# An mLSTM cell and a leaky-ReLU MLP on one core: another order at the start of each MLP group, an earlier weight load, and weight sums at other places

## The chip, the cores and the metric

The kernel runs on one core of a Trainium2 chip. A core has several engines that run side by side, each with its own queue in program order: PE (TensorE, matrix products; its weight loads are shown as PEld), DVE (VectorE), ACT (ScalarE), POOL (GpSimd) and SP (SyncE, which here only issues DMAs; ACT issues some too). They hand work to each other through semaphores. Data lie in SBUF, products in PSUM, the inputs and the output in device memory (HBM).

The metric is the device time of one execution in microseconds (us); the median of several executions counts. One further execution was recorded by the hardware profiler; all times inside the kernel are from it.

## The reference

Two blocks in a row, all in float32. The first is an mLSTM cell over 4 batches, 8 heads, 768 steps, 40 values per head. The second multiplies its output, as 3072 rows of 320, by two matrices with a leaky ReLU between them.

```python
for t in range(S):                       # first block
    m_new = np.maximum(f_gate[:, :, t] + m, i_gate[:, :, t])
    f_stab = np.exp(f_gate[:, :, t] + m - m_new)
    i_stab = np.exp(i_gate[:, :, t] - m_new)
    C = f_stab[..., None, None] * C + i_stab[..., None, None] * np.einsum('bhd,bhe->bhde', vt, kt)
    n = f_stab[..., None] * n + i_stab[..., None] * kt
    denom = np.maximum(np.abs(np.einsum('bhd,bhd->bh', n, qt)[..., None]), 1.0)
    y[:, :, t] = sigmoid(o_gate[:, :, t]) * np.einsum('bhde,bhe->bhd', C, qt) / denom
x = y.transpose(0, 2, 1, 3).reshape(3072, 320)
h = x @ w_in                             # second block: 320 x 2048
out = np.maximum(0.01 * h, h) @ w_out    # 2048 x 320
```

## The kernel before

**Chunks and groups.** The 768 steps are cut into 6 chunks of 128. Within a chunk the cell is computed with matrix products, batch by batch; one batch of one chunk is called a cell here, numbered s = 4 * chunk + batch. What the cells of chunk g give (4 batches x 128 steps = 512 rows of x) is the input of MLP group g. The main loop (variable `c`, 1 to 6) runs the products of group c - 1 and, between them, the cells of chunk c. It steps through 28 products for a group from 1 on (index `i`); after each product it lets other work in. The queues of PE, DVE, ACT and POOL hold exactly the order in which this loop calls things; a planner places only SP's DMAs.

**The cell's visits.** A cell visits PE twice: `u_parts` (scores `sd`, lines 629 and 634, followed on DVE by L639 and L610) and `u_mix` (product `pT`, L710, followed by a row on DVE and POOL: L717, L648 to L650, L721 on DVE, L724 on POOL, L728 on DVE). The list `pairs` says after which `i` the visits of two cells come. Before its visits a cell needs its mask added (`prep_mask`, POOL L453), exponentials (`prep_exp`, ACT L461), transposes and products of k and q (`prep_kq`, DVE L516 and L524), and steps of the state on POOL (L606, L481). The gates of the next chunk are scanned on DVE (`gates`, L283 to L303) and put through exponentials on ACT (`gates_exp`, L314 and L315).

**The fast groups.** Groups 1 to 5 use a scheme that replaces 8 block products by 7 with sums of blocks. For the first layer (`fast_firsts`) the blocks are those of x (b11, b12, b21, b22; b12 and b22 hold the second half of the rows) and of w_in. The products are p1, p6, p7, p4, p2, p5, p3, each for n = 0 and 1. p1, p6 and p7 have two terms, the others three. A product accumulates in two PSUM banks; p1, p6, p7, p4 follow each other in the same banks ("u"), p2 has its own ("s"), p5 and p3 share a third pair ("v"). After a product ACT copies the banks to `acts` (L979) or DVE adds them to it (L975), and ACT applies the leaky ReLU (L971). A product that goes on in a bank has to wait until this reading is over. Group 1 alone has p2 ahead of p1 (`swapped`). The sums of x (`sums_of_x`) are 12 instructions on POOL (L928). The sums of w_in (`sums_of_weights`) are 14 on DVE (L908 to L911, L918), once.

The second layer (`fast_units`, L830) has its own seven products, also called p1 to p7, in the order p1, p2, p4, p6, p7, p5, p3. They use four sums of blocks of w_out (`mixed_weights`, POOL L203 to L206, 128x1280 each), made once, in group 1. In this document p1 to p7 mean the first layer's products unless the second layer is named.

**Weights.** w_in and w_out come from HBM as 64-bit words, two eighths or quarters at a time, into a staging area, and are narrowed to float32 by seven instructions (`narrow_weights`: ACT L251, then DVE L253 to L267). The last eighth of w_out is loaded at `i` = 15 of c = 1 into a part of the staging area that an earlier eighth used.

Of the kernel before, what the change touches and what calls it, by code (L numbers as in the profile page):

```python
# [10 lines left out]
U32 = mybir.dt.uint32  # L11
# [7 lines left out]
def kernel(  # L19
# [176 lines left out]
    x4_at = raw_l[:, at + 12 * P : at + 12 * P + 2 * HT].rearrange("p (k t) -> p k t", t=HT)  # L196
    p1_at = [raw_l[:, at + 12 * P + 2 * HT + n * NH :][:, :NH] for n in range(2)]

    def mixed_weights():

        a11, a12, a21, a22 = low_w[:, :, :NH], low_w[:, :, NH:], high_w[:, :, :NH], high_w[:, :, NH:]
        t2, t3, t4 = t_at
        yield nc.gpsimd.tensor_tensor(t3, a22, a12, op=ALU.subtract)  # L203
        yield nc.gpsimd.tensor_tensor(a12, a12, a11, op=ALU.subtract)
        yield nc.gpsimd.tensor_tensor(t2, a22, a12, op=ALU.subtract)
        yield nc.gpsimd.tensor_tensor(t4, a21, t2, op=ALU.subtract)  # L206

    def load_weights(n):

        m = n - QN  # L210
        if n < QN:
            dst = w_in[:, n, :]
        else:
            dst = w_out[:, 2 * m : 2 * m + 2, :].rearrange("p a d -> p (a d)")
        to = dst
        if wide:
            if n < 2:
                at = NF * GT - 2 * WC * (n + 1)
                raw = acts_l[:, at : at + 2 * WC].bitcast(U64)
            elif n < QN:  # L220
                raw = raw_t[:, WC * (n - 2) : WC * (n - 1)]
            elif m < 2:
                raw = w_out[:].rearrange("p f d -> p (f d)")[:, (2 + m) * WC : (3 + m) * WC].bitcast(U64)
            else:
                at = (4, 0, 1, 2, 3, 4)[m - 2] * HW
                raw = raw_t[:, at : at + HW]
            raws[n] = (raw, dst)
            to = raw
        if n < QN:
            src = moe_w_in[:, n * QC : (n + 1) * QC].rearrange("(k p) (r c) -> r p k c", p=DP, r=2)  # L230
            for slot in range(KC):
                for r in range(2):
                    nc.sync.dma_start(  # L233
                        to[DP * r : DP * (r + 1), 2 * P * slot : 2 * P * (slot + 1)], src[r, :, SLOTS[r][slot], :],
                    )
        else:
            rows = moe_w_out[2 * m * P : 2 * (m + 1) * P, :]
            nc.sync.dma_start(to.rearrange("p (a d) -> p a d", d=Dm), rows.rearrange("(a p) d -> p a d", p=P))

    def narrow_weights(n):  # L240
# [6 lines left out]
        words = raw.bitcast(U32).rearrange("p (c two) -> p c two", two=2)  # L247
        lo, hi = words[:, :, 0], words[:, :, 1]
# [671 lines left out]
    def sums_of_x(g):  # L920

        xT = st["xT", g]
        for what in range(4):
            for rows, k, a, b in alike:
                b11, b12, b21, b22 = (xT[rows, j, ts(i, HT)] for j in (a, b) for i in range(2))
                x2, x3, x4 = (t[rows, k] for t in (x2_at, x3_at, x4_at))
                to, left, right = ((x3, b22, b12), (b12, b12, b11), (x2, b22, b12), (x4, b21, x2))[what]
                nc.gpsimd.tensor_tensor(to, left, right, op=ALU.subtract)  # L928

    def fast_firsts(g):  # L930
# [50 lines left out]
        swapped = g == 1  # L981

        def p1(n):
            z = at(n, 0, 0)
            bank = product(n, list(zip(w_at(0, n, K1), x_at(K1, 0))), ("u", n))
            if swapped:
                add(z, bank)
                relu(z, z)
            else:
                keep(z, bank)  # L990
# [7 lines left out]
        def p4(n):  # L998
            bank = product(n, list(zip(w_at(1, n, K2), t_of(x4_at))) + rest(1, n, 0), ("u", n))
# [3 lines left out]
        def p2(n):  # L1003
            z = at(n, 0, 0)
            bank = product(n, list(zip(w_at(0, n, K2), x_at(K2, 0))) + rest(0, n, 0), ("s", n))
            if swapped:
                keep(z, bank)
            else:
                add(z, bank)
                relu(z, z)  # L1010

        def p5(n):
            z = at(n, 1, 1)
            add(z, product(n, list(zip(w_at(1, n, K1), x_at(K1, 1))) + rest(1, n, 1), ("v", n)))
# [7 lines left out]
        order = (p2, p1, p6, p7, p4, p5, p3) if swapped else (p1, p6, p7, p4, p2, p5, p3)  # L1022
        return [lambda p=p, n=n: p(n) for p in order for n in range(2)]
# [23 lines left out]
    def ahead(s):  # L1047

        if s < NS:
            if s < 2 * B:  # L1050
                u_split(s)
            if s >= 2 * B:
                late[s] = 5 if 2 * B + 2 <= s < 3 * B else 3
# [114 lines left out]
    with tc.manual_schedule(engines={E.PE, E.DVE, E.Activation, E.Pool}):  # L1168
# [23 lines left out]
        for c in range(1, NB + 1):  # L1192
# [6 lines left out]
            for i in range(n_ff):  # L1199
# [102 lines left out]
```

## Time and profile before

| | |
|---|---|
| median of 3 executions | 502.8 us (502.01 to 503.71) |
| profiled execution | 496.93 us |
| its span, first to last instruction | 495.1 us |
| mean granted PE clock | 0.972 |
| PE busy | 480.3 us (97%) |
| DVE busy | 353.7 us (71%) |
| ACT busy | 203.7 us (41%) |
| POOL busy | 199.8 us (40%) |
| HBM traffic | 118 GB/s over the span |

Busy time is the time in which an engine executes instructions; waits and DMA issues are not counted. The profile's windows cut the span into stretches and give each engine's busy time in them, with the clock that PE was granted (1.00 is full). The list of waits says who waited for whom. The order of time lists instructions with start and length; "x3" are three in a row under one line.

The five fast groups start at 138.78, 216.89, 288.20, 359.45 and 430.17 us in the span. Ahead of them lie the first chunk's cells, the narrowing of the weights and group 0.

### The profile page before, as it was taken

Reading aid. Unit: us, or ns where it says so; the run is one execution under the profiler, and the core shown is the slowest. Engines: PE = TensorE matmul, PEld = TensorE weight load, DVE = VectorE, ACT = ScalarE, POOL = GpSimd, SP = SyncE. Lnnn points to the kernel's source line nnn. Section 1 sums busy time; section 2 is a strip of 40 time slices with the busy share of each in tenths; the row PEclk is TensorE's granted clock in tenths of the full one; section 3 lists DMA queues with packets and bytes.
Section 4 is the critical chain, followed back from the end, with each engine's and each line's share of the span. In section 5 each row is a group of like instructions: output and inputs, shape, how many; then the busy total and the mean of one; then the engine's idle time right before and its main releaser. Section 6 shows DMA issues by size and latency. Waiting matters only on the chain.

```text
span 495.1 us, 14022 instructions
## 1 busy us (share of the span) xinstructions
PE 480.3 (97%) x5621; PEld 433.5 (88%) x5621; DVE 353.7 (71%) x585; ACT 203.7 (41%) x508; POOL 199.8 (40%) x239
## 2 busy tenths in 40 slices
PE   8997999999998899999999999999999999999997
PEld 7896788867787789998899998899989899988997
DVE  4759998898999967786787886787737787104641
ACT  3465865742635351155631335620344611153210
POOL 4142743452385961494412694203583003700020
PEclk9568999999999989999999999999999999999999
DMA  9977786898761573486584685663865211200001
GB/s 115 161 193 160 168 209 163 173 187 169 158 142 26 135 149 80 115 167 151 145 152 96 150 170 118 174 124 93 156 161 128 54 56 46 87 1 1 2 1 54
DMA packets 165297, 59.31 MB, mean 120 GB/s; under 512 B 128816, under 2 KB 156016, under 8 KB 165232
## 3 DMA queue, kind: packets, MB, share of 16 engines
q1 hardware_dynamic: 125104, 51.20, 46.0%
q10 hardware_dynamic: 40128, 7.21, 9.2%
q8 instruction: 44, 0.72, 0.6%
q14 instruction: 21, 0.17, 0.1%
HBM read 51.68 MB, written 6.70 MB: 118 GB/s over the span
## 4 chain that ended last, share of the span: by engine, by line
PE 70%; DVE 11%; SPq 9%; DMA 4%; ACT 3%; issue 2%; POOL 0%; ACTq 0%; DVEq 0%; POOLq 0%
PE po L830 31%; PE ph L946 27%; SPq L233 4%; PE pT L710 3%; PE sd L629 2%; PE po L796 2%; SPq L358 2%; PE ph L774 2%; DVE qn L524 1%; SPq L372 1%; DVE qn L639 1%; ACT kqT L554 1%; PE sd L634 1%; DMA w<-a_dr 1%; DMA rb<-in_q_dram 1%
## 5 line engine op out<-in xcount | busy, mean ns | idle before, releaser
L830 PE MATMUL po<-w_out,acts 128*128 128x160 f32 x640 | 89.1, 300 | 0.0
L830 PEld LDWEIGHTS po<-w_out,acts 128*128 128x128 f32 x640 | 87.3, 190 | 0.6 <-ACT acts L971 0.3
L946 PE MATMUL ph<-xT,w_in 64*128 64x256 f32 x720 | 82.7, 378 | 0.0
L946 PEld LDWEIGHTS ph<-xT,w_in 64*128 64x128 f32 x720 | 69.2, 187 | 8.9 <-issue 0.7
L975 DVE TENSOR_TENSOR acts<-acts,ph 128x512 f32<-128x512 f32 x60 | 38.3, 682 | 41.6 <-PE ph L946 41.5
L830 PE MATMUL po<-raw,acts 128*128 128x160 f32 x480 | 66.4, 300 | 0.0
L830 PEld LDWEIGHTS po<-raw,acts 128*128 128x128 f32 x480 | 65.4, 190 | 0.3
L606 POOL TENSOR_TENSOR S<-S,f 40x336 f32<-40x336 f32 x36 | 31.6, 879 | 75.7 <-PE pT L710 35.9
L461 ACT ACTIVATE w<-w,gT 128x64 f32<-128x64 f32 (+1 forms) x192 | 51.7, 346 | 15.7 <-DMA w<-a_dr 4.6
L979 ACT COPY acts<-ph 128x512 f32<-128x512 f32 x60 | 32.1, 587 | 46.7 <-PE ph L946 46.7
L971 ACT ACTIVATE acts<-acts 128x1024 f32<-128x1024 f32 x30 | 31.7, 1056 | 43.6 <-DVE acts L975 43.4
L774 PE MATMUL ph<-xT,w_in 64*128 64x256 f32 x320 | 38.6, 392 | 1.2 <-ACT acts L782 1.2
L946 PE MATMUL ph<-acts,w 64*128 64x256 f32 x320 | 37.5, 382 | 1.8 <-DVE acts L975 1.8
L453 POOL TENSOR_TENSOR w<-w,i 128x512 f32<-128x512 f32 x20 | 27.7, 1394 | 26.2 <-DMA w<-a_dr 14.3
L774 PEld LDWEIGHTS ph<-xT,w_in 64*128 64x128 f32 x320 | 31.6, 193 | 5.7 <-ACT acts L782 1.6
L796 PE MATMUL po<-w_out,acts 128*128 128x320 f32 x128 | 36.5, 437 | 0.0
L946 PEld LDWEIGHTS ph<-acts,w 64*128 64x128 f32 x320 | 31.2, 187 | 5.7 <-POOL w L453 2.2
L724 POOL TENSOR_TENSOR xb<-xb,den 128x320 f32<-128x320 f32 x16 | 11.6, 727 | 60.5 <-DVE xb L721 58.1
L639 DVE TENSOR_TENSOR qn<-w,sd 64x512 f32<-64x512 f32 x40 | 27.3, 684 | 8.2 <-PE sd L629 4.5
L796 PEld LDWEIGHTS po<-w_out,acts 128*128 128x128 f32 x128 | 23.6, 190 | 9.3 <-issue 0.3
L863 POOL TENSOR_TENSOR y<-y,raw 128x160 f32<-128x160 f32 x10 | 9.5, 950 | 54.5 <-DVE acts L865 44.0
L946 PE MATMUL ph<-xT,raw 64*128 64x256 f32 x240 | 29.0, 394 | 1.7 <-DVE acts L975 1.7
(169 smaller groups left out, 810.8 us busy)
## 6 DMA issues: line engine op xcount, KB each, us to landing
rb<-in_k_dram SPq DMA_DIRECT2D x64, 80.0 KB
rb<-in_q_dram SPq DMA_DIRECT2D x64, 80.0 KB
rb<-in_o_gate_dram SPq DMA_DIRECT2D x64, 80.0 KB
ea<-a_dr SPq DMA_DIRECT2D x32, 128.0 KB
raw<-in_moe_w_out_dram SPq DMA_DIRECT2D x6, 640.0 KB
w<-a_dr ACTq DMA_DIRECT2D x24, 128.0 KB
xT<-x_dr SPq DMA_DIRECT2D x32, 96.0 KB
acts<-in_moe_w_in_dram SPq DMA_DIRECT2D x20, 128.0 KB
```

What stands on the lines that cost most here:

```text
L233: nc.sync.dma_start(to[DP * r : DP * (r + 1), 2 * P * slot : 2 * P * (slot + 1)], src[r, :, SLOTS[r][slot], :],)
L453: nc.gpsimd.tensor_tensor(w, w, cm2.unsqueeze(1).to_broadcast([P, H, SL]), op=ALU.add)
L461: yield nc.scalar.activation(w[:, h, :], w[:, h, :], AF.Exp, bias=gT[c][:, 0, bh : bh + 1], scale=1.0)
L606: nc.gpsimd.tensor_tensor(new, old, g, op=ALU.mult)
L639: nc.vector.tensor_tensor(mixed(s)[toks, u], w[toks], bank[1 - u][toks], op=ALU.mult)
L774: nc.tensor.matmul(ph[r][:, cols], lhsT=w_row(r, slot, j), rhs=xT[DP * r : DP * (r + 1), slot, cols], start=(slot == 0), stop=(slot == KC ...
L796: nc.tensor.matmul(po[n][:], lhsT=acts[:, f, ts(n, P)], rhs=w_out[:, f, :], start=(f == 0), stop=(f == NF - 1),)
L830: nc.tensor.matmul(bank[:], lhsT=left[:, f, :], rhs=right[:, f, :], start=f == 0, stop=f == KH - 1)
L946: nc.tensor.matmul(bank[r][:, e, :], lhsT=left(r)[rows, e], rhs=right(r)[rows], start=first and e == 0 and m == 0, stop=e == 1 and m == le ...
L971: nc.scalar.activation(to, z, AF.Prelu, alpha=0.01)
L975: nc.vector.tensor_tensor(to[:, 2 * r : 2 * r + 2], to[:, 2 * r : 2 * r + 2], bank[r], op=ALU.add)
L979: nc.scalar.copy(to[:, 2 * r : 2 * r + 2], bank[r])
```

## The change

- The last eighth of w_out is loaded at `i` = 11 instead of 15, into the unused upper halves of `w_all`, as two DMAs of half the columns each. `narrow_weights` follows with a three-dimensional view.
- All fast groups begin with p2, then p1; p2 is copied by ACT and p1 added by DVE. Before, this held for group 1 alone.
- The sums of x write b12 - b11 to an area of its own (`x1_at`) instead of over b12, in another order, nine ahead of the group. The last three (b21 minus a sum, over b21) are issued behind p2(1) (`last_sum_of_x`), since p2 reads b21.
- The first two cells' `u_parts` come at `i` = 0 instead of 1; `gates` at `i` = 3 and `gates_exp` at 4 for all chunks from the third (c = 3 and later had 0 and 2). The masks of the third and fourth cell move from `i` = 0 to 4.
- The mixed weights of w_out: three of the four stay on POOL, at `i` = 0 (two) and 1 of group 1 instead of from 10 on; the fourth (a12 - a11) goes to DVE at `i` = 18.
- The last two sums of w_in (L918) come behind the gates of group 1.
- ACT's slow DMA issues (`chores`) start at `i` = 8, one per product, and two per product from 14. The steps of `prep_kq` go one per product up to 13 and two after it, in all groups.

```diff
-    x4_at = raw_l[:, at + 12 * P : at + 12 * P + 2 * HT].rearrange("p (k t) -> p k t", t=HT)
+    x1_at = raw_l[:, at + 12 * P : at + 12 * P + 2 * HT].rearrange("p (k t) -> p k t", t=HT)
...
         yield nc.gpsimd.tensor_tensor(t3, a22, a12, op=ALU.subtract)
-        yield nc.gpsimd.tensor_tensor(a12, a12, a11, op=ALU.subtract)
-        yield nc.gpsimd.tensor_tensor(t2, a22, a12, op=ALU.subtract)
+        yield nc.gpsimd.tensor_tensor(t2, t3, a11, op=ALU.add)
         yield nc.gpsimd.tensor_tensor(t4, a21, t2, op=ALU.subtract)
+        yield nc.vector.tensor_tensor(a12, a12, a11, op=ALU.subtract)
...
+            elif m == NF // 2 - 1:
+                raw = w_all[:, :, H * SL :].bitcast(U64)[:, :, : HW // NL]
+                dst = dst.rearrange("p (n c) -> p n c", n=NL)
...
-                at = (4, 0, 1, 2, 3, 4)[m - 2] * HW
+                at = (4, 0, 1, 2, 3)[m - 2] * HW
...
+            if len(to.shape) == 3:
+                n = NL // 2
+                for a in range(2):
+                    nc.sync.dma_start(to[:, n * a : n * (a + 1), :], rows[ts(a, P), :].rearrange("p (n c) -> p n c", n=n))
+                return
...
-        for what in range(4):
+        for what in range(3):
             for rows, k, a, b in alike:
-                b11, b12, b21, b22 = (xT[rows, j, ts(i, HT)] for j in (a, b) for i in range(2))
-                x2, x3, x4 = (t[rows, k] for t in (x2_at, x3_at, x4_at))
-                to, left, right = ((x3, b22, b12), (b12, b12, b11), (x2, b22, b12), (x4, b21, x2))[what]
+                b11, b12, b22 = xT[rows, a, :HT], xT[rows, a, HT:], xT[rows, b, HT:]
+                x1, x2, x3 = (t[rows, k] for t in (x1_at, x2_at, x3_at))
+                to, left, right = ((x1, b12, b11), (x2, b22, x1), (x3, b22, b12))[what]
                 nc.gpsimd.tensor_tensor(to, left, right, op=ALU.subtract)
+
+    def last_sum_of_x(g):
+
+        for rows, k, a, b in alike:
+            b21 = st["xT", g][rows, b, :HT]
+            nc.gpsimd.tensor_tensor(b21, b21, x2_at[rows, k], op=ALU.subtract)
...
-        order = (p2, p1, p6, p7, p4, p5, p3) if swapped else (p1, p6, p7, p4, p2, p5, p3)
-        return [lambda p=p, n=n: p(n) for p in order for n in range(2)]
+        return [lambda p=p, n=n: p(n) for p in (p2, p1, p6, p7, p4, p5, p3) for n in range(2)]
...
-                late[s] = 5 if 2 * B + 2 <= s < 3 * B else 3
+                late[s] = 5 if s % B > 1 else 3
...
-        fetch = {4: (3, 4), 8: (5, 6), 15: (7,)}
+        fetch = {4: (3, 4), 8: (5, 6), 11: (7,)}
...
-        masks = {0: (2, 3), 12: (4, 5)}
-        pairs = (1, 1, 4, 4, 13, 13, 17, 17, 17)
-        sums = sums_of_weights()
+        masks = {4: (2, 3), 12: (4, 5)}
+        pairs = (0, 0, 4, 4, 13, 13, 17, 17, 17)
+        sums, mixes = sums_of_weights(), mixed_weights()
...
-                for _ in range(1 if c > 2 and i < N1 else 2 if i > 5 else 0):
+                for _ in range(1 if i < N1 else 2):
...
-                if c == 1 and i >= 24:
+                if c == 1 and 24 <= i < 28:
                     run(sums, 3)
-                if c == 2 and i == 10:
-                    mixes = mixed_weights()
-                if c == 2 and i >= 10:
-                    next(mixes, None)
+                if c == 2 and i in (0, 1, 18):
+                    run(mixes, 2 if i == 0 else 1)
...
-                if chores and (c != 2 or i > 6):
+                for _ in range(0 if i < 8 else 1 if i < N1 else 2):
                     while chores and next(chores[0], chores) is chores:
                         chores.pop(0)
                 if c + 1 < NB:
-                    if i == (1, 3, 0)[min(c, 3) - 1]:
+                    if i == (1 if c == 1 else 3):
                         gates(c + 1)
-                    if i == (3, 4, 2)[min(c, 3) - 1]:
+                        if c == 2:
+                            run(sums)
+                    if i == (3 if c == 1 else 4):
                         gates_exp(c + 1)
```

More of the change, by code (lines that the diff above doesn't have):

```diff
@@ L246, in narrow_weights @@
         raw, dst = raws.pop(n)
-        words = raw.bitcast(U32).rearrange("p (c two) -> p c two", two=2)
-        lo, hi = words[:, :, 0], words[:, :, 1]
+        words = raw.bitcast(U32)
+        if len(words.shape) == 3:
+            words = words.rearrange("p n (c two) -> p n c two", two=2)
+            lo, hi = words[:, :, :, 0], words[:, :, :, 1]
+        else:
+            words = words.rearrange("p (c two) -> p c two", two=2)
+            lo, hi = words[:, :, 0], words[:, :, 1]
         d = dst.bitcast(U32)
@@ L979, in keep @@
                 nc.scalar.copy(to[:, 2 * r : 2 * r + 2], bank[r])
-        swapped = g == 1
         def p1(n):
             z = at(n, 0, 0)
[L985 to L990, printed above, removed]
+            add(z, product(n, list(zip(w_at(0, n, K1), x_at(K1, 0))), ("u", n)))
+            relu(z, z)
         def p6(n):
@@ L998, in p4 @@
         def p4(n):
-            bank = product(n, list(zip(w_at(1, n, K2), t_of(x4_at))) + rest(1, n, 0), ("u", n))
+            bank = product(n, list(zip(w_at(1, n, K2), x_at(K2, 0))) + rest(1, n, 0), ("u", n))
             for r in range(2):
@@ L1003, in p2 @@
         def p2(n):
[L1004 to L1010, printed above, removed]
+            keep(at(n, 0, 0), product(n, list(zip(w_at(0, n, K2), x_at(K2, 0))) + rest(0, n, 0), ("s", n)))
+            if n == 1:
+                last_sum_of_x(g)
         def p5(n):
             z = at(n, 1, 1)
-            add(z, product(n, list(zip(w_at(1, n, K1), x_at(K1, 1))) + rest(1, n, 1), ("v", n)))
+            add(z, product(n, list(zip(w_at(1, n, K1), t_of(x1_at))) + rest(1, n, 1), ("v", n)))
             relu(z, z)
```

## The prediction

> **What bounds the kernel now.** I read in this order: the share of each engine on the page (PE 97%), the windows cut at the starts of the five fast groups, the list of what PE waited for, and then the order of time of PE, DVE, POOL and ACT in the one group that is too long. The windows first. The columns after the stretch are its length, then busy time of PE, PEld, DVE, ACT and POOL, the granted clock, the DMA share and GB/s.
>
> ```profile
> 138.78:216.89 78.11, 74.60 (x905) 68.16 (x904) 65.47 (x100) 27.57 (x71) 49.46 (x45) 0.98 0.51 117
> 216.89:288.20 71.31, 71.31 (x904) 66.60 (x904) 55.33 (x93) 28.25 (x74) 31.98 (x39) 1.00 0.65 139
> 288.20:359.45 71.25, 71.25 (x905) 66.55 (x904) 55.10 (x92) 27.48 (x70) 29.02 (x36) 1.00 0.65 137
> 359.45:430.17 70.72, 70.72 (x834) 66.49 (x834) 43.14 (x72) 22.55 (x50) 26.59 (x36) 1.00 0.36 90
> 430.17:492.11 61.94, 61.91 (x513) 58.18 (x512) 19.37 (x28) 17.29 (x30) 6.78 (x11) 1.00 0.03 12
> ```
>
> Groups 2 to 5 have PE busy from end to end, and the change leaves the number of matmuls as it is. So nothing is to be won there; only lost. Group 1 (138.78 to 216.89) has the same matmuls as group 2 and takes 78.11 - 71.31 = 6.8 us more. That is all the change can gain behind 138.78. Ahead of it PE has no gap from 105.21 to 149.95. PE's largest wait is that of group 1:
>
> ```profile
> PE ph L946 <- DVE acts L975: 3.5, 2, 1.8
> ```
>
> The two gaps are 1.81 us ahead of p6(0) at 151.75 and 1.71 us ahead of p3(0) at 173.72. Both times DVE adds a bank (L975) too late for the next product into that bank. The second is followed by a stretch at half clock:
>
> ```profile
> 146.22:151.75 5.53, 3.73 (x36) 3.04 (x33) 5.45 (x9) 0.00 (x0) 5.22 (x7) 1.00 0.12 42
> ...
> 170.76:174.17 3.41, 1.70 (x14) 1.07 (x10) 3.38 (x3) 0.04 (x1) 3.31 (x2) 1.00 0.71 158
> 174.17:177.58 3.41, 3.41 (x18) 2.66 (x18) 1.28 (x3) 3.29 (x8) 0.00 (x0) 0.50 0.63 173
> ```
>
> Half clock over 3.41 us costs 1.7 us. The rest of the 6.8 us is the gaps and the first product behind each, slowed because its second bank is still being added.
>
> Why DVE is late at 172.97 is read from DVE and POOL side by side (start, length, instruction):
>
> ```profile
> 164.45 1.87 DVE L524 TENSOR_TENSOR qn<-kqT,ea 64x512 f32<-64x512 f32 x2
> 166.35 1.31 DVE L516 STREAM_TRANSPOSE kqT<-rb 128x512 f32<-128x512 f32 x2
> 167.69 5.26 DVE L524 TENSOR_TENSOR qn<-kqT,ea 64x512 f32<-64x512 f32 x2
> 172.97 2.48 DVE L975 TENSOR_TENSOR acts<-acts,ph 128x512 f32<-128x512 f32 x4
> ```
>
> ```profile
> 165.73 3.35 POOL L203 TENSOR_TENSOR raw<-w_out 128x1280 f32<-128x1280 f32 x1
> 169.16 3.23 POOL L204 TENSOR_TENSOR w_out<-w_out 128x1280 f32<-128x1280 f32 x1
> ```
>
> The same pair L524 takes 1.87 us in one place and 5.26 under the mixed weights. Each of its halves ends just behind a POOL instruction. A DVE instruction that reads two tensors of SBUF waits here until the POOL instruction in flight is over. The adds and L639, which read PSUM, do not (L975 takes its 0.62 each under L453). Even the 32x1 step of the gates is held: 0.68 us behind a sum of x in group 2, where it takes 0.14 alone in group 1.
>
> ```profile
> 220.38 0.68 DVE L299 TENSOR_TENSOR m<-m,m 32x1 f32<-32x1 f32 x1
> ```
>
> **The change part by part** (all in the profiled execution: span 495.1, its own time 496.93, which is 5.9 under the median 502.8; I carry the difference over).
>
> *Last eighth of w_out.* ACT sat 8.9 us at L251 until its transfer landed at 121.6, and DVE then idled 1.53 us (120.97 to 122.50). Issued as two transfers some 3 to 11 us sooner, it is there before DVE asks. SP issues one DMA more (about 0.6 us, row L238 0.54); behind it stand loads with several us to spare. PE is full here, so the worth is 0 directly. But the sums of the weights end sooner: 145.00 - 1.53 = 143.5.
>
> *Group 1 up to p6(0).* L918 (2.26) moves behind the gates. Visits come after p2(0): PE 138.78 + 2.61 (one product of three terms) + 2.1 (two visits) = 143.5, p2(1) to 146.1, p1(0) to 147.85, p1(1) to 149.6 (1.74 each). DVE does the four L639 and two L610 (3.7) from 143.5 to 147.2, waits for p1(0), and adds it by 149.1. p6(0) starts at 149.6 with no gap. Before, p1 ended at 149.95 and p6(0) at 154.19, that is 4.24 for a product of 1.74: 2.5 us gained here.
>
> *POOL.* First sum at 137.84 as before (it waits for ACT's copy). Five under DVE's sums at 1.09 (rows L928: 137.84 to 143.31), four at 0.73: 146.2. Then the two moved weight sums: 2.92 each, which L205 and L206 took with DVE out of the way: 152.2. Then three last sums of x, each letting one DVE gate step through (0.87 a turn, as at 217 to 221): 154.8. The fourth weight sum: 157.8. Only then masks and the visits' work. Before, masks were over at 152.71.
>
> *Gates and DVE.* p1(1) is added by 150.9. The gates meet POOL's queue: first step behind 152.2, three between the last sums, L299 behind the long one at 157.8, L303 at 158.0. L918's two halves go behind one mask each (1.27 + 0.55 a turn): 161.45. So L717 of the first mix starts at 161.45, not 155.38: 6.07 later. From L717 to the add took 17.59 us before; the slow pair of 5.26 is now behind the add: 12.33. The add starts at 161.45 + 12.33 = 173.8 against 172.97, **0.8 later**. So p3(0) starts near 174.5. Lower end: if L717 is not held, POOL's product for the mix (masks over at 160.9, L606 0.77) is the limit, which gives 172.1, and with POOL undisturbed 171.0. Upper end: one more turn of 1.2 lost: 175.0. I take 173.8, since each turn copies a measured one.
>
> *ACT and p7(1).* The exponentials of the gates (L314) stand ahead of the copy of p6(1) on ACT and need L303: 158.0 + 0.24 + 0.33 + 0.81 (L497) + 0.59 = 160.0. PE would be at p7(1) at 156.85 (p6(0) 151.3, mixes 2.02 to 153.35, p6(1), p7(0)). A **new gap of 3.1 us**. Then p7(1) 1.74 and four products at 2.61: PE is through p5(1) at 172.2, still 2.3 ahead of p3(0). The new gap is thus paid from time that PE would have waited anyway.
>
> *Clock.* A gap of 1.71 brought half clock here, one of 1.81 did not. A gap of 3.1 is the likelier to bring it. If it does, 1.7 us are lost ahead of p5(1), inside the 2.3 of slack, and the gap at p3(0) shrinks to 0.6, too short to bring another. p3 then runs at full clock: 174.5 + 0.55 (second bank) + 5.23 (208 matmuls in 22.65, 48 of them) = 180.3, where before it ended at 181.36. **-1.1 us.**
>
> *Fourth weight difference on DVE* (1280 wide, between the second-layer steps): 1.21 us for 1024 (L848), so 1.5, up to 3 behind a POOL instruction. DVE has 0.4 to 2.3 us of idle in each 5 us from 190 to 210 and its reader is the sixth of seven product kinds: 0. Without that cover it would be the 1.5.
>
> *Groups 2 to 5.* p1's add moves from the second half to where p6(0) waits for it: 1.28 of adding under 1.74 of p1(1), margin 0.46, DVE free since 7.5 us into the group and p1(0) over at 9.0. Gates now on the path of p6(1)'s copy: 16.2 against 16.3 us into the group, p7(1) at 18.0. Last sums of x: POOL waits for p2(1) at 7.3, done at 9.5, needed at 19.8. The masks queue behind them, over at 12, first visit's product not before 13.5. Two DMA issues on ACT per product from the fourteenth on: 2 x 0.6 + 0.3 in 2.2 us. Sum 0, with up to 0.5 a group if a margin fails.
>
> **Sum:** -1.1, from 496.93 to 495.8 profiled, 502.8 to 501.7.
>
> **The rivals.**
> *POOL's long sums do not hold the small gate steps* (they slip in between): add at 171.0 to 172.1, p7(1) little delayed, p3(0) at 171.7 to 172.8, with full clock over at 177.5 to 178.6: -2.8 to -3.9, about 499.4. For it: L303 went straight behind L299 at 220.99. Against it: L299 itself waited.
> *Both gaps closed*: -6.8, 496.0. Against it: the POOL queue above.
> *Slower: the clock falls at the second gap.* The gap at p7(1) leaves the clock alone, as 1.81 us did, and the one at p3(0) of 2.3 brings it down, as 1.71 did: p3 takes its 7.64 of before from 174.5: 182.1, +0.8; with the add at its upper end +2.0, 503.6 to 504.8. It decides from p3(0) at 173.7 on, if the half clock still follows.
> The Trainium skill, "TensorE: Matmul & The Clock Gate", section "Why this matters for your kernels", asks for no PE-idle gaps above about 3 us. By that rule the second gap brings no half clock and the first may: -1.1 again, and the slower case falls away. This trace disagrees with it once, at 1.71 us, so I keep that case.
> *Margins in groups 2 to 4 fail* (p6(0) or p7(1)): 0.5 to 1.5 each, +1 to +4 with the rest, about 504. Against it: PE full there and DVE at 77%.
>
> **How the numbers follow.** Forecast 0.36; small steps slip in 0.27; both gaps closed 0.07; clock falls at the second gap 0.2; margins fail 0.1. 0.3% is 1.5 us, about what can be told from no change. Faster: 0.27 + 0.07 and a part of the forecast's case (p3(0) up to 0.9 sooner), 0.09: 0.43. Slower: half of the clock case, the margins, 0.04 for a late POOL: 0.24. The rest, 0.33, is within. The range leaves out the closed gaps and the far end of the margins: 498.4 to 504.6; the forecast's own is 500.8 to 502.6.
>
> **What would show it.** Right: no PE gap ahead of p6(0); ACT's copy of p6(1) waiting on DVE, with a PE gap near 157 to 160; the 1280-wide POOL sums at 146 to 158; L299 held for some 2.5 us; p3(0) within 1 us of 173.7; group 1 near 77 us; groups 2 to 5 at 71.3, 71.25, 70.7, 61.9. Wrong: L717 of the first mix before 158, or PE gaps in groups 2 to 4, or a changed start of group 1.

## The result and the profile after

The changed kernel takes 503.93 us (median of 22 executions, 501.3 to 507.82), the kernel before in the same comparison 499.07 (22 executions, 494.27 to 504.44). The ratio is 1.0117 with a 95% interval of 1.0091 to 1.0142: slower by 1.2%, some 4.9 us by the medians. The forecast was 501.7 us and a gain of 1.1. The number lies in the stated range of 498.4 to 504.6, the sign is wrong. That the number lies there is luck: the base of 502.8, from 3 executions, was high (in later comparisons the kernel before had medians from 497.6 to 501.1). As a change against its base the range was -4.4 to +1.8 us, and +4.9 lies outside it.

The profiled execution has a span of 500.8 us and a mean granted clock of 0.966, against 495.1 and 0.972. The windows of the changed kernel, cut at the starts of its five fast groups (columns as in the prediction):

```profile
141.31:222.45 81.14, 75.10 (x904) 69.77 (x903) 69.16 (x101) 28.11 (x73) 45.97 (x44) 0.96 0.56 120
222.45:293.74 71.29, 71.29 (x904) 66.60 (x903) 54.90 (x94) 27.23 (x70) 32.18 (x39) 1.00 0.64 139
293.74:364.98 71.24, 71.24 (x903) 66.55 (x902) 54.81 (x92) 27.41 (x70) 28.83 (x37) 1.00 0.62 136
364.98:435.54 70.56, 70.56 (x834) 65.92 (x833) 43.67 (x72) 22.47 (x50) 26.66 (x37) 1.00 0.32 86
```

Groups 2 to 4 are what they were (71.31, 71.25, 70.72 before). Group 1 grew from 78.11 to 81.14 instead of shrinking to 77. It also starts 2.53 us later. In this pair of profiles that is start-up: between 73 and 82 us, where both kernels issue the same instructions, PE has two gaps of 0.94 and 0.70 us in the changed kernel, followed by 3.41 us at half clock, and one of 0.32 us without half clock in the kernel before. From 105.2 us on (107.7 in the changed kernel) to the start of group 1 both take the same 33.6 us.

What PE waited for in group 1 (who waits, for whom; us in total, times, longest):

```profile
PE ph L965 <- ACT acts L990: 5.6, 1, 5.6
PE po L843 <- DVE acts L892: 0.3, 1, 0.3
```

The two gaps of before, both for DVE's adds, have become one, and it is for ACT: p5(1) takes over the banks of p4(1), whose leaky ReLU (L990) is late. ACT's order of time says why (start, length, instruction, idle time before it):

```profile
164.82 1.09 ACT L990 ACTIVATE acts<-ph 128x512 f32<-128x512 f32 x2 [1.46 <-PE ph L965]
174.78 0.53 ACTq L1083 DMA_DIRECT2D w<-a_dr  x1
175.35 1.09 ACT L990 ACTIVATE acts<-ph 128x512 f32<-128x512 f32 x2 [9.44 <-DMA x_dr<-x]
```

In the kernel before, the second slow issue stood ahead of the same ReLU and held it for far less:

```profile
167.98 1.08 ACT L971 ACTIVATE acts<-ph 128x512 f32<-128x512 f32 x2 [2.63 <-DMA rb<-in_o_gate_dram]
```

In the changed kernel p4(1) ends on PE near 167.5. Its ReLU starts at 175.35, because the first slow DMA issue (L1083) stands ahead of it and waits until 174.7. What it waits for is a write of x by SP, put down in the trace as a semaphore that both DMAs use. The DMAs of these kernels share eight semaphores in turn, and each issue waits until the last DMA on its semaphore has landed:

```
start          queue  DMA                      semaphore
167.68-168.79  SP     x_dr<-x, first visit     107 108 100 102
171.58-173.08  SP     x_dr<-x, second visit    103 104 105 106
174.78         ACT    w<-a_dr (L1083)          waits on 106 and 102, takes 106
```

So ACT, and behind it PE, waits for the x of the second visit, which DVE makes. DVE is late because of POOL:

```profile
149.50 2.91 POOL L203 TENSOR_TENSOR raw<-w_out 128x1280 f32<-128x1280 f32 x1
152.49 2.92 POOL L204 TENSOR_TENSOR raw<-raw,w_out 128x1280 f32<-128x1280 f32 x1
155.37 2.34 POOL L947 TENSOR_TENSOR xT<-xT,acts 128x256 f32<-128x256 f32 x3
157.78 3.77 POOL L205 TENSOR_TENSOR raw<-w_out,raw 128x1280 f32<-128x1280 f32 x1
161.51 2.94 POOL L466 TENSOR_TENSOR w<-w,i 128x512 f32<-128x512 f32 x2
```

```profile
157.97 0.14 DVE L312 TENSOR_TENSOR m<-m,m 32x1 f32<-32x1 f32 x1
158.04 0.14 DVE L316 TENSOR_TENSOR na<-m,F 32x1 f32<-32x1 f32 x1
158.11 3.98 DVE L931 TENSOR_TENSOR raw<-w_in 64x512 f32<-64x512 f32 x2
162.13 0.72 DVE L730 STREAM_TRANSPOSE hb<-pT 128x512 f32<-128x512 f32 x1
...
175.97 1.28 DVE L994 TENSOR_TENSOR acts<-acts,ph 128x512 f32<-128x512 f32 x2
```

The second half of L931 (the last two sums of w_in) is held until L205 ends: it takes 3.30 us, the first half 0.67. The first mix (L730) starts 20.8 us into the group. Before it was L717, 16.6 us into the group:

```profile
155.38 0.72 DVE L717 STREAM_TRANSPOSE hb<-pT 128x512 f32<-128x512 f32 x1 [0.37 <-PE pT L710]
```

The add of p5(0), for which p3(0) waits, comes 34.7 us into the group (before: 34.2). Then the clock. Windows of one clock step each, columns as above:

```profile
170.21:173.62 3.41, 0.17 (x1) 0.00 (x0) 3.08 (x5) 0.00 (x0) 3.10 (x5) 1.00 0.12 30
173.62:177.04 3.42, 1.04 (x4) 1.01 (x6) 3.36 (x5) 1.09 (x2) 0.44 (x1) 0.50 0.66 159
177.04:180.45 3.41, 3.41 (x19) 3.16 (x17) 0.81 (x2) 2.82 (x9) 0.00 (x0) 0.50 0.71 167
```

In the two windows at half clock PE works 4.45 us, which costs half of that, 2.2.

### The profile page after: what moved, and what is told of

Its sections match the earlier page's. It is cut to its first block, busy times and chain, and to the rows that moved or that the text cites. A ratio compares the mean times of both kernels' runs of the same rounds, so it can differ in the third digit from the quotient of the medians.

```text
span 500.8 us, 14043 instructions
## 1 busy us (share of the span) xinstructions
PE 481.8 (96%) x5621; PEld 436.9 (87%) x5621; DVE 359.1 (72%) x586; ACT 202.7 (40%) x508; POOL 195.8 (39%) x238
## 4 chain that ended last, share of the span: by engine, by line
PE 75%; DVE 9%; SPq 7%; DMA 4%; ACT 2%; issue 1%; POOL 0%; ACTq 0%; DVEq 0%; POOLq 0%
PE ph L965 29%; PE po L843 29%; PE po L809 6%; SPq L236 3%; PE sd L642 3%; PE ph L787 3%; PE pT L723 3%; SPq L371 2%; DMA w_out<-in_moe_w_out_dram 1%; SPq L385 1%; PE sd L647 1%; DMA x_dr<-x 1%; DVE raw L931 1%; DMA w<-a_dr 1%; DVE raw L278 1%
## 5 line engine op out<-in xcount | busy, mean ns | idle before, releaser
L965 PE MATMUL ph<-xT,w_in 64*128 64x256 f32 x720 | 88.3, 380 | 0.0
L965 PEld LDWEIGHTS ph<-xT,w_in 64*128 64x128 f32 x720 | 72.9, 188 | 8.3 <-issue 0.7
L990 ACT ACTIVATE acts<-acts 128x1024 f32<-128x1024 f32 x30 | 31.7, 1056 | 32.4 <-DVE acts L994 32.3
L466 POOL TENSOR_TENSOR w<-w,i 128x512 f32<-128x512 f32 x20 | 28.8, 1450 | 38.3 <-DMA w<-a_dr 37.8
L787 PE MATMUL ph<-xT,w_in 64*128 64x256 f32 x320 | 39.5, 399 | 0.9 <-ACT acts L795 0.9
L787 PEld LDWEIGHTS ph<-xT,w_in 64*128 64x128 f32 x320 | 32.3, 198 | 5.8 <-ACT acts L795 1.3
L809 PE MATMUL po<-w_out,acts 128*128 128x320 f32 x128 | 36.5, 436 | 0.0
L965 PE MATMUL ph<-raw,w_in 64*128 64x256 f32 x160 | 25.0, 401 | 5.6 <-ACT acts L990 5.6
```

What stands on the lines that cost most here:

```text
L466: nc.gpsimd.tensor_tensor(w, w, cm2.unsqueeze(1).to_broadcast([P, H, SL]), op=ALU.add)
L787: nc.tensor.matmul(ph[r][:, cols], lhsT=w_row(r, slot, j), rhs=xT[DP * r : DP * (r + 1), slot, cols], start=(slot == 0), stop=(slot == KC ...
L809: nc.tensor.matmul(po[n][:], lhsT=acts[:, f, ts(n, P)], rhs=w_out[:, f, :], start=(f == 0), stop=(f == NF - 1),)
L965: nc.tensor.matmul(bank[r][:, e, :], lhsT=left(r)[rows, e], rhs=right(r)[rows], start=first and e == 0 and m == 0, stop=e == 1 and m == le ...
L990: nc.scalar.activation(to, z, AF.Prelu, alpha=0.01)
```

## The experiments

Group 1 is measured from its first product to the first of group 2, in one profile of each kernel; by that measure it takes 78.03 us before and 81.13 after. The times are ratios to the kernel before in the same comparison.

**1. The slow DMA issue.** It moves behind the ReLU of p4(1), or one product further ahead.

```diff
-                for _ in range(0 if i < 8 else 1 if i < N1 else 2):
+                for _ in range(0 if i < 9 else 1 if i < N1 else 2):
```

> The changed kernel, with ACT's slow DMA issues starting at i = 9 instead of 8, so that the first issue (L1083) stands behind the leaky ReLU of p4(1) instead of ahead of it. Theory 1 (the issue holds ACT): in the changed kernel L1083 waits until 174.7 for the write of x of the second visit, whose semaphore it shares; the ReLU of p4(1) waits behind it and p5(1), which takes over that bank, behind the ReLU. Then here the gap of 5.62 us ahead of p5(1) is gone (under 0.5), PE waits instead at p3(0) for DVE's add of p5(0) (over at 35.9 us into the group in the changed kernel), and group 1 takes 77.7 to 79.5 us instead of 81.14; the time is 1.7 to 3.4 us under the changed kernel's. Theory 2 (the ReLU is late for another reason, POOL or DVE, and the issue only stands beside it): the gap stays within 1 us of 5.6 and group 1 at 80 to 81.5.

Measured: ratio 1.0060 (1.0029 to 1.0091), 501.29 us, 2.6 under the changed kernel by the medians; the two intervals together leave some 1 to 5 us. PE's wait in group 1 has changed its owner:

```profile
PE ph L965 <- DVE acts L994: 3.8, 1, 3.8
```

The gap ahead of p5(1) is gone, and the 3.77 us are ahead of p3(0), which starts 35.9 us into the group. That is where the prediction had it (35.7). Group 1 took 80.42 us in this profile, only 0.7 less than in the changed kernel and above the 77.7 to 79.5 expected, since the clock was at half for two steps here too, from 174.38 to 181.20, with 5.76 us of PE's work in them: 2.9 us lost. The mechanism of theory 1 holds; the worth is small, because the next wait stands right behind it.

```diff
-                for _ in range(0 if i < 8 else 1 if i < N1 else 2):
+                for _ in range(0 if i < 7 else 1 if i < N1 else 2):
```

> The changed kernel, with ACT's slow DMA issues starting at i = 7, as in the kernel before. Theory 1: the first issue now stands ahead of the ReLU of p4(0) and takes the semaphore of the last write of x of the first visit (landing near 29 us into the group), the second stands ahead of the ReLU of p4(1) and takes that of a load behind all the writes of x (landing near 33.5). So one gap becomes two: some 3 us ahead of p5(0) and some 2 ahead of p5(1), p5(1) starts within 1 us of where it did, and group 1 stays at 80 to 82 us: starting the issues later was not the error by itself, the late writes of x are. Theory 2: no gap ahead of p5(0); the gap ahead of p5(1) as in the changed kernel.

Measured: ratio 1.0050 (1.0017 to 1.0084), 501.2 us.

```profile
PE ph L965 <- ACT acts L990: 3.9, 1, 3.9
```

The wait is now ahead of p5(0) (3.86 us at 170.77), as theory 1 says and theory 2 does not. The second gap that I expected did not show: p5(0), at half clock, ran in the time for which the second issue holds p5(1). Group 1 took 79.75 us, a little under the 80 to 82, and the time is that of the kernel with the issues from 9 on, where I had expected the changed kernel's: a miss. As I read it, ahead of p4(0)'s ReLU the wait comes out of what PE loses to p3(0) anyway; only at i = 8, where it holds p5(1) until p3(0) could have begun, does it add to the time. Only the two places were run, not this explanation of their difference.

**2. The mixed weights late again.**

```diff
-                if c == 2 and i in (0, 1, 18):
-                    run(mixes, 2 if i == 0 else 1)
+                if c == 2 and i in (10, 11, 18):
+                    run(mixes, 2 if i == 10 else 1)
```

> The changed kernel, with the three mixed weights of POOL at i = 10 (two) and 11 instead of 0 and 1. Theory 1: they hold DVE's L931 (3.30 for one half) and the masks, and so the first mix (L730) starts 20.8 us into the group where it was 16.6 before. Without them L730 starts 15.5 to 17.5 us into the group, the writes of x end 3 to 5 us sooner, the gap ahead of p5(1) falls from 5.62 to under 2, and group 1 takes 77 to 79 us. Theory 2 (the mix is late because of the sums of x and the gates ahead of it, not the mixed weights): L730 stays past 19 us, the gap at 4 us or more, and group 1 over 80.

Measured: ratio 0.9931 (0.9893 to 0.9970), 495.78 us: 8.2 under the changed kernel, and faster than the kernel before. Its group 1 as a window, and DVE in it:

```profile
142.52:215.45 72.93, 72.56 (x903) 67.06 (x902) 61.34 (x99) 27.97 (x73) 45.59 (x44) 1.00 0.61 133
```

```profile
157.30 1.37 DVE L931 TENSOR_TENSOR raw<-w_in 64x512 f32<-64x512 f32 x2
158.70 0.72 DVE L730 STREAM_TRANSPOSE hb<-pT 128x512 f32<-128x512 f32 x1
...
171.02 1.29 DVE L994 TENSOR_TENSOR acts<-acts,ph 128x512 f32<-128x512 f32 x2
```

L931 takes 1.37 us instead of 3.98, the first mix starts 16.2 us into the group and the add of p5(0) 28.5 us into it, 6.2 sooner. The DMA issue is still at i = 8, and ACT is idle for 3.50 us ahead of p4(1)'s ReLU, but PE no longer waits for it. PE has no gap over 0.3 us in the group and the clock stays up. Group 1 is 8.2 us shorter (81.13 to 72.93), more than the 2 to 4 expected: I had not reckoned that the second gap and the half clock both go.

Both edits together:

> Both edits: mixed weights from i = 10, slow DMA issues from i = 9. Theory 1: nothing stands ahead of the ReLU of p4(1), and the first mix is early: no gap ahead of p5(1), at p3(0) one of 0 to 2.5 us (the mixed weights then lie beside prep_kq's pair, as they did in the kernel before), group 1 at 75.5 to 78 us, 3 to 5.5 us under the changed kernel and 0 to 3 under the kernel before in the same stretch. Theory 2: as for the single edits, a gap stays and group 1 is over 79.

Measured: ratio 0.9937 (0.9902 to 0.9971), 495.17 us, group 1 73.56. Shorter than the 75.5 to 78 expected, and no better than the mixed weights alone: with x in time the place of the issue is worth nothing.

**3. The early mixed weights alone, in the kernel before.** In this kernel the fourth mixed sum is computed behind the second-layer product that reads it.

```diff
-                if c == 2 and i == 10:
-                    mixes = mixed_weights()
-                if c == 2 and i >= 10:
-                    next(mixes, None)
+                if c == 2 and i == 0:
+                    mixes = mixed_weights()
+                if c == 2 and i in (0, 1, 18):
+                    run(mixes, 2 if i == 0 else 1)
```

> The kernel before, with one part of the change alone: the mixed weights of w_out on POOL at i = 0 (two), 1 and 18 of group 1 instead of from 10 on. Theory 1 (the early mixed weights are what makes the changed kernel slower, by holding DVE's steps that read two SBUF tensors and POOL's work for the mixes): the gates and the first mix meet three POOL instructions of about 3 us, L717 moves from 16.6 us into group 1 to 20 to 25, the gap ahead of p3(0) grows, and group 1 takes 81 to 86 us instead of 78.03; the time is 0.6% to 1.6% above the kernel before. Theory 2 (they hurt only together with the other moves of the change): L717 stays under 18.5 and group 1 at 77 to 79.

Measured: ratio 1.0288 (1.0217 to 1.0359), 511.67 us, far above the 0.6% to 1.6% expected, and group 1 above its 81 to 86 us. Part of it belongs to the edit's last step: a gap of 6.29 us for the fourth sum (L206) in the second layer, also followed by half clock. Without that gap group 1's 89.90 us are 83.6 or less. L717 starts 24.9 us into the group, as theory 1 says. DVE's steps of the gates end one by one with the POOL instructions (L203 ends at 159.36, L204 at 162.34, L205 at 165.31):

```profile
157.92 1.72 DVE L283 TENSOR_TENSOR_SCAN F<-fi,zeros 32x128 f32<-32x128 f32 x1
159.56 2.85 DVE L286 TENSOR_SCALAR il<-fi,m 32x128 f32<-32x128 f32 x1
162.45 3.13 DVE L289 TENSOR_TENSOR_SCAN m<-fi,il 32x128 f32<-32x128 f32 x1
```

The gap ahead of p3(0), expected to grow, is gone, because PE now waits earlier: 3.55 us ahead of p6(0), with two steps at half clock, and 1.64 us ahead of p7(1) for ACT's copy of p6(1), which stands behind the exponentials of the held gates. This second wait is the one that the prediction had placed in the changed kernel:

```profile
PE ph L946 <- ACT acts L979: 1.6, 1, 1.6
```

**4. How many of them.** The third of the sums is put off, two stay early.

```diff
-                if c == 2 and i in (0, 1, 18):
+                if c == 2 and i in (0, 10, 18):
```

> The changed kernel, with only the third mixed weight (L205) put off, to i = 10; the first two stay at i = 0. Group 1 took 81.13 us with all three early and 72.93 with none. Theory 1 (what counts is the one that runs while DVE comes to L931 and the mix, L205 at 16.5 to 20.2 us into the group): L931 meets only two masks, L730 starts at 17.5 to 19 us instead of 20.81, the gap ahead of p5(1) falls from 5.62 to 2 or less, and group 1 takes 74 to 77 us, more than half of the 8.2 us won back by one of three. Theory 2 (every us of POOL ahead of the masks costs the same): a third is won back, group 1 takes 78 to 79 us and L730 starts past 19.

Measured: ratio 1.0048 (1.0011 to 1.0085), 499.94 us. L730 starts 19.6 us into the group, the gap ahead of p5(1) is 2.64 us, group 1 takes 79.54. Theory 1 of this run fails: the third sum is not the one that counts, 1.6 of the 8.2 us came back in the profile and 4.0 by the medians. Theory 2 is nearer, but the loss is no straight line either: the gap halves (5.62 to 2.64), while two steps at half clock still follow, with 6.1 us of PE's work in them, 3.1 lost.

**5. The pace of prep_kq**, taken back in the kernel of experiment 2 to that of before:

```diff
-                for _ in range(1 if i < N1 else 2):
+                for _ in range((2 if i > 5 else 0) if c == 2 else 1 if i < N1 else 2):
```

> The changed kernel with the mixed weights from i = 10 (group 1 in 72.93 us), and the steps of prep_kq in group 1 at the pace of the kernel before (none up to i = 5, two per product after it, instead of one per product up to 13). Theory 1 (the gap of the kernel before ahead of p3(0) came from the second prep_kq pair standing ahead of DVE's add of p5(0) and running under the mixed weights, and the slower pace is what took it away): the add of p5(0) moves from 28.5 us into the group to 31 to 34, a gap of 1 to 3 us comes back ahead of p3(0), group 1 takes 74.5 to 77.5 us. Theory 2 (the pace does nothing, the rest of the change is enough): the add stays within 1 us and group 1 under 73.7.

Measured: ratio 1.0064 (1.0028 to 1.0100), 500.89 us. The add of p5(0) is again behind the second pair, which again takes 5.24 us under the mixed weights:

```profile
169.41 5.24 DVE L537 TENSOR_TENSOR qn<-kqT,ea 64x512 f32<-64x512 f32 x2
174.68 2.48 DVE L994 TENSOR_TENSOR acts<-acts,ph 128x512 f32<-128x512 f32 x4
```

It starts 34.0 us into the group, a gap of 2.83 us stands ahead of p3(0), group 1 takes 76.84: theory 1, within its numbers. The same part alone in the kernel before:

```diff
-                for _ in range(1 if c > 2 and i < N1 else 2 if i > 5 else 0):
+                for _ in range(1 if i < N1 else 2):
```

> The kernel before, with one part of the change alone: the steps of prep_kq go one per product up to i = 13 in groups 1 and 2 too. Theory 1 (of what the change gains in group 1 the most comes from this: DVE's adds of p5 come ahead of the second prep_kq pair's long halves, which run under the mixed weights): the add of p5(0), 34.2 and 36.1 us into the group in the two profiles of the kernel before, moves to 29 to 32, no gap over 0.5 us ahead of p3(0), the one ahead of p6(0) stays, group 1 takes 74 to 77.5 us instead of 78.03 and 80.09, and the time is 0.4% to 0.9% under the kernel before. Theory 2 (it needs the earlier first mix as well): the add stays past 33, group 1 over 77.5 and the time within 0.3%.

Measured: ratio 0.9924 (0.9887 to 0.9961), 497.45 us. No gap ahead of p3(0), group 1 77.19 us. The add came 34.0 us into the group, not at 29 to 32: in this profile the gap ahead of p6(0) was 3.55 us and the first mix came at 19.9 instead of 16.6, so all behind it shifted. The gain is as theory 1 says, the number of the add was missed.

**6. The last two sums of w_in**, ahead of the visits again, in the kernel of experiment 2:

```diff
-                if c == 1 and 24 <= i < 28:
+                if c == 1 and i >= 24:
```

> The changed kernel with the mixed weights from i = 10, and the last two sums of w_in (L931) back ahead of group 1's first visits, as in the kernel before. Theory 1 (they stood ahead of the add of p1 and made the gap ahead of p6(0)): the add of p1(0) moves from 9.66 us into the group to 11.2 to 12.4, a gap of 0.7 to 2 us comes back ahead of p6(0), and group 1 takes 73.4 to 75 us instead of 72.93. Theory 2 (the earlier visits alone closed that gap): no gap over 0.3 us ahead of p6(0), group 1 within 0.4 us of 72.9.

Measured: ratio 0.9983 (0.9948 to 1.0018), 496.45 us; no gap ahead of p6(0), group 1 72.06 us. Theory 1 fails: moving L918 behind the gates closed nothing; the gap went because of the other moves around the start of the group. In group 1 of these two profiles the move cost 0.9 us (72.93 to 72.06), but by the ratios this kernel is slower than that of experiment 2, not faster (0.9983 against 0.9931, intervals overlapping), so the cost is not shown by the times. The time did not follow in this profile, since a gap of 2.24 us at 121 and two steps at half clock made the group start at 144.74. That gap is the next subject.

**7. The last eighth of w_out**, loaded as before, in the kernel of experiment 2:

```diff
-            elif m == NF // 2 - 1:
-                raw = w_all[:, :, H * SL :].bitcast(U64)[:, :, : HW // NL]
-                dst = dst.rearrange("p (n c) -> p n c", n=NL)
...
-                at = (4, 0, 1, 2, 3)[m - 2] * HW
+                at = (4, 0, 1, 2, 3, 4)[m - 2] * HW
...
-        fetch = {4: (3, 4), 8: (5, 6), 11: (7,)}
+        fetch = {4: (3, 4), 8: (5, 6), 15: (7,)}
```

> The changed kernel with the mixed weights from i = 10, and the last eighth of w_out loaded as in the kernel before (one transfer, at i = 15 of group 0, into its old area). Theory 1 (the part is a loss: its second transfer is issued at 115.27 us where the single one was at 115.18, and since it goes into the tile of the masks' weights, DVE's L652 of the last visit ahead of group 1 waits for it, 0.5 to 3.5 us in seven of eight profiles): no wait of L652 for that transfer, no PE gap over 0.3 us at 118 to 124 us, group 1 starts at 138.5 to 141.5 us and the time is 0.3 to 1.5 us under that of the kernel with the mixed weights from 10 alone (495.8). Theory 2 (the part changes nothing, the gaps there come from the start-up): PE gaps at 118 to 124 us stay, the time is within 0.3 us or above.

Measured: ratio 0.9892 (0.9841 to 0.9942), 494.09 us, group 1 from 139.47 on, no PE gap between 106 and 200 us. What DVE and PE waited for at 100 to 138 us in the kernel of experiment 2, where the load is the new one:

```profile
DVE qn L652 <- DMA w<-in_moe_w_out_dram: 2.2, 1, 2.2
...
PE hN L693 <- DVE qn L652: 1.0, 1, 1.0
```

Both lines are gone here. Over all profiles: with the new load (eight kernels) group 1 starts at 139.58 to 144.74 us, median 141.1; with the old one (six) at 138.08 to 141.63, median 139.2. A part of that is start-up. Counted from PE's transposes of the gates (`tg`), 104.5 to 107.7 us into the span, group 1 starts 33.6 us later in four of the six with the old load and in one of the eight with the new, the changed kernel. The other two with the old load take 34.7 and 36.5; these issued it last, at 117.5 and 118.8 us, and PE waited for its narrowing. The other seven with the new load take 34.1 to 39.7. The medians are 34.6 against 33.6. The new load is not sooner either. Its first half is issued at 105.8 to 109.7 us, but its second at 114.0 to 116.5, where the old one is issued at 114.3 to 118.8; and from that last issue to ACT's narrowing pass 8.5 to 9.2 us instead of 5.6 to 7.5. The intervals of the two ratios overlap, so it is the wait and the starts that show the loss, of about 1 us.

Both repairs together:

> As m_raw, and the last two sums of w_in (L931) ahead of group 1's first visits, as in the kernel before. That alone took group 1 from 72.93 to 72.06 us, but with a gap of 2.24 us for the late transfer in that profile. If the two edits are independent, group 1 takes 71.8 to 72.6 us with no gap at 118 to 124, and the time is 0.5 to 2 us under 495.8, 3 to 5 under the kernel before. If the sums push DVE's later work into the gap of p6(0), group 1 is over 73.

Measured: ratio 0.9871 (0.9825 to 0.9917), 493.40 us, group 1 from 138.91 on in 72.64 us. The best median: 1.3% under the kernel before. Against experiment 2 it is 2.4 us by the medians, but the two intervals overlap. It keeps of the change the order of the products, the earlier visits, the split sums of x, the later masks and gates, the slow DMA issues from i = 8 on, the fourth mixed sum on DVE and the slower pace.

**8. The kernel before, once more.**

> The kernel before, unchanged, for a second profile: nine kernels with the same instructions in the first 75 us began group 1 at 138.78 to 144.74 us. If that spread is the start-up's own (clock steps and load times), group 1 here starts anywhere from 139 to 142.5 us and not at 138.8 again, and group 1 itself takes 77 to 79.5 us.

Measured: group 1 from 138.08 on, sooner than expected, and 80.09 us long, above the 77 to 79.5:

```profile
138.08:218.17 80.09, 76.29 (x903) 69.32 (x902) 65.74 (x100) 28.15 (x72) 49.68 (x46) 0.96 0.51 114
```

The same two gaps (2.12 and 1.68 us) brought half clock twice here, once in the first profile. Single profiles of one kernel differ by 2 us in group 1, 1.7 of it through the second step at half clock; terms of that size need the times beside them.

**The account.** By medians the change is +4.9. From the changed kernel on, one part after the other taken back: the early mixed weights are +8.2 (experiment 2), the new load +1.7 (495.78 to 494.09), L931 +0.7 (494.09 to 493.40); what is left gains 5.7 (499.07 to 493.40), most of it through the pace of prep_kq. By the ratios the same steps are 1.9, 0.4, 0.2 and -1.3 percentage points, in sum the 1.2. Either sum closes by construction, since its terms are differences of neighbouring versions; it is no test. The medians come from several comparisons, so each term is good to about 1 us at best: the mixed weights and the gain of the rest are clear of that, the load rests on the waits shown above, and L931 on group 1 of two pairs of profiles alone (72.93 to 72.06, and 73.31 to 72.64).

## Why the prediction was wrong, point by point

**Right.** That group 1 decides, and that groups 2 to 4 stay (71.29, 71.24, 70.56; the rest of the span 65.27 against 65.03). No gap ahead of p6(0). The sums of 1280 on POOL about 1 us behind the place foreseen, counted from the group's start. That POOL's long sums hold DVE's work (shown by experiments 2 and 3). The add of p5(0): predicted 35.0 us into the group, measured 34.7; with the DMA issue out of the way p3(0) came at 35.9, predicted 35.7. That the add fits so well is in part luck: the first mix came 1.9 us sooner than predicted (20.8 us into the group, not 22.7), and from there to the add took 13.8 us, not 12.3, mainly because L662 took 1.19 us beside a mask and not 0.18.

**Wrong: L299 held and the gap at p7(1).** The gates' last steps (L299 and L303 before, L312 and L316 now) took 0.14 us each at 157.97 and 158.04, with L205 already begun at 157.78; only L931 was held by it. That is the mechanism of the rival in which the small steps slip in between, though not its time. The copy of p6(1) was done by 161.5, and PE had no gap over 0.14 us there (p6(1) to p7(1) took 5.74 us for 5.23 of work). So the 3.1 us of waiting that I had placed ahead of p7(1), to be taken off the later gap, stayed with the later one. By its own sign, L717 of the first mix before 158 would have told against the forecast; it came at 162.13, of which 2.53 are the later start.

**Wrong: ACT's slow DMA issues at nothing.** This step and the next, the clock, are what made the forecast fail. I costed them as two issues of 0.6 us per product from the fourteenth on, and did not ask what the first, moved from behind the copies of p7(1) to behind the ReLU of p4(0), waits for and what stands behind it. It shares a semaphore with the x of the visit that I had just worked out to be late. It made the gap of 5.62 us ahead of p5(1). Its price, net of the wait behind it, is 2.6 us by the medians and 0.7 in group 1 of the profiles (experiment 1). So it does not carry the whole miss: without it the kernel is still slower than before.

**Wrong: the clock.** "p3 then runs at full clock" rested on the gap at p7(1) taking up the wait and the half clock falling into slack. In the changed kernel it fell on 4.45 us of PE's work, 2.2 us. With the DMA issue out of the way PE waited 3.77 us at p3(0), not 0.6, and the half clock behind that gap cost 2.9 us. There p3 ended 44.4 us into the group, where 41.5 was predicted (180.3 less 138.78): the 2.9 us are the whole difference in that profile. In the changed kernel it ended 45.2 us into the group. The rival "the clock falls at the second gap" had this mechanism, and the first kernel of experiment 1 is its case. I gave it 0.2 and priced it at +0.8 to +2.0; by medians that kernel is 2.9 us over the kernel before.

**Wrong: the last eighth "is there before DVE asks".** DVE still waited for ACT's narrowing (1.4 us in the changed kernel, 1.5 before), so the sums of w_in ahead of the first visits ended 6.0 us into the group, not 4.7. In seven of the eight profiles with the new load it also put a wait on the masks' tile that I had not looked for.

**Mis-sized: the mixed weights.** I charged them, net of the slow pair that moves behind the add, with 0.8 us at p3(0). Against the kernel without them they cost 8.2, because I compared with the kernel before, whose p5 add was late for another reason that the change removes. Without them the add comes 28.5 us into the group, not 34, and the rival "both gaps closed", to which I gave 0.07, is what happens.

## What to carry to other kernels

When a DMA issue moves on an engine that also computes, look up which semaphores it waits on and which late transfer used them last: everything behind it in that queue, and every bank those instructions free, inherits the wait. A bulk job on POOL belongs where DVE has no chain of two-input SBUF steps on the path; here three sums of 3 us at the wrong end of a group cost 8 us, and the useful parts together gained 6. Weigh each part of a bundle against the kernel with the other parts in, not against the kernel before: a delay that another part would have removed hides the price of this one.

## What the runs showed of the hardware

**Half clock follows the idle share of a fixed step, not the length of a gap.** All changes of the granted clock lie on a grid of 3.41 us. From 48 us on, over the profiles of all these kernels, 9 of the 10 full-clock steps in which PE was idle for 56% or more were followed by a step at half clock, 5 of the 8 between 48 and 53%, and none of those below 47%. One gap of 1.71 us inside one step (idle 50%) brought it in the kernel before. A gap of 2.83 us that straddles two steps did not, in the kernel of experiment 5:

```profile
170.48:173.89 3.41, 2.12 (x18) 1.54 (x14) 3.38 (x2) 1.54 (x6) 3.33 (x2) 1.00 0.73 182
173.89:177.30 3.41, 1.87 (x14) 1.46 (x16) 3.24 (x5) 1.30 (x3) 3.33 (x2) 1.00 0.67 156
177.30:180.70 3.40, 3.40 (x36) 3.05 (x33) 1.28 (x2) 3.40 (x11) 1.62 (x3) 1.00 0.65 173
```

A gap of 2.64 us that falls mostly into one step did, in the kernel of experiment 4:

```profile
169.54:172.95 3.41, 1.47 (x12) 0.96 (x8) 3.31 (x5) 0.00 (x0) 3.25 (x4) 1.00 0.37 91
172.95:176.37 3.42, 2.72 (x11) 2.56 (x13) 2.76 (x5) 2.03 (x6) 2.25 (x1) 0.50 0.79 195
```

The first figure after the length is PE's busy time. This is found in the traces, not tested by a run that only shifts a gap. It would explain why the same kernel pays for nearly the same gap in one execution and not in the next (2.12 and 1.81 us ahead of p6(0), in the two profiles of the kernel before). The Trainium skill, "TensorE: Matmul & The Clock Gate", section "Why this matters for your kernels", puts the limit at PE-idle gaps of about 3 us; the runs differ from it on the short side.

**DVE waits for whole POOL instructions.** A step of 32x128 took 3.13 us beside a 1280-wide sum and 0.41 in experiment 2. A step with one tensor and a column of values (L286) was held as well, 2.85 us against 0.25 in the kernel before. It is no strict turn-taking: in the changed kernel three gate steps and the first half of L931 ran between 157.77 and 158.79, although L205 is recorded from 157.78 on; L205 then took 3.77 us instead of 2.9. The Trainium skill, "SBUF — State Buffer", section "Who interferes with whom", says that a DVE instruction with two SBUF inputs contends with a POOL instruction that reads SBUF, and that the port pair they share is locked exclusively; the traces agree, with these lengths.
